# Four attention layers in one kernel: unit ends in pairs, outputs scaled in place, narrower masks, and unread matmuls in the final layer

## The chip, the cores and the metric

The kernel runs on one core of a Trainium2 chip. The time is that of the device, in microseconds, from one launch. It is compared by the median of several runs; a profile is one further execution, with its own time.

## What is computed

Four layers in a row work on x, of 2048 rows and 640 columns, in bfloat16. Each adds to x an attention over 32 heads of 20 columns, of x normalized by row. Layers 0 and 2 (weights A) let a row see itself and the 255 rows before it; layers 1 and 3 (weights B) let it see all 2048.

```python
def _A_ref(x, wqkv, wo):
    B, S, D = x.shape
    H = 32; Dh = D // H; W = 256
    qkv = (lambda x, *d: x.transpose(*d))((x @ wqkv).reshape(B, S, 3, H, Dh), 2, 0, 3, 1, 4)
    q, k, v = qkv[0], qkv[1], qkv[2]
    scores = jnp.einsum("bhqd,bhkd->bhqk", q, k) * (Dh ** -0.5)
    idx = jnp.arange(S)
    mask = (idx[:, None] - idx[None, :] >= 0) & (idx[:, None] - idx[None, :] < W)
    scores = jnp.where(mask[None, None], scores, -1e9)
    p = _softmax(scores, axis=-1)
    o = jnp.einsum("bhqk,bhkd->bhqd", p, v)
    return (lambda x, *d: x.transpose(*d))(o, 0, 2, 1, 3).reshape(B, S, D) @ wo
...
x = A_x
x = x + _A_ref(_layernorm(x, axis=-1), A_wqkv, A_wo)
x = x + _B_ref(_layernorm(x, axis=-1), B_wqkv, B_wo)
x = x + _A_ref(_layernorm(x, axis=-1), A_wqkv, A_wo)
x = x + _B_ref(_layernorm(x, axis=-1), B_wqkv, B_wo)
return x
```

`_B_ref` is the same without the mask.

## The kernel before, in words

**Units.** The 2048 queries are cut into four chunks of 512, the 32 heads into eight groups of four. A unit is one layer, chunk and group. A head's 20 columns lie in a strip of 32 partitions, so that four heads' scores (L1298) run side by side on TensorE's rows. Scores stand with keys on the partitions and queries on the columns, one bank of PSUM (512 columns) for each block of 128 keys and each head. In a layer with a window a bank holds two or more such blocks, those of the keys that the chunk can see (`window_banks`), and there is one bank for each of three patterns and each head.

**Tiles.** Banks of successive units are taken three at a time, now and then two or four: a tile. For each tile TensorE writes the scores, ScalarE takes the exponential of all its banks in one instruction (L1329) into `pt`, VectorE multiplies windowed banks by a mask of zeros and ones (L1399), and two or three tiles later TensorE multiplies by the values (L1363) into one bank, `op`. The values have a column of ones, so `op` holds, for each of four heads, 20 rows of sums and one row with the sum of the exponentials. Two halves of PSUM take turns: tile t uses banks 0 to 2, tile t+1 banks 3 to 5 or, with four, 3 to 6.

For a few banks of layers 1 and 3 the exponential is worked out on VectorE instead, in some twelve steps (`t_side`, L904 to L949).

**The end of a unit.** When the last value product of a unit is issued, `finish_unit` copies `op` to a tile `oT` in bfloat16 (L863, VectorE) and starts `t_tail`. This picks the sums with four small matmuls (L1044), takes reciprocals (L1049), splits each into a high and a low bfloat16 part (L1053, L1054), transposes them (L1061), copies the result (`rT`, L1063), spreads it over the partitions with four matmuls against `spread4` (L1072), and multiplies `oT` by it into `on` (L1079), which holds a chunk's eight groups. `require` forces work forward where something needs it.

**Projection.** When all groups of a chunk are done, `t_out` multiplies `on` with `wo` (L558) and adds to x (L567). With `packed`, here all of layer 3, `nu` is first moved by small copies on SyncE's queue (L1090) from strips of 32 to dense rows of 20, so that five matmuls do the work of eight. The last chunk of layer 3 does its first six groups apart (`t_before_last`) and the last two in the end. `load_wop` loads `wo`, dense or in strips, when the layer that projects changes.

**The order.** All engines take their instructions in an order that the program writes out, tile by tile. After a tile's scores and exponential are issued, `pump` issues as much of the waiting work as a credit allows: normalization (`t_ln`), projections of q, k and v (L370, L471), unit ends (`tails`, always first) and output projections. Such a piece takes one free bank of PSUM from `take_m`, and a wait of ("wait", n) lets n tiles pass. From layer 1 on that bank is mostly bank 6 alone. Units of layers 1 and 2, and 2 and 3, are interleaved; from chunk 1 of layer 3 on there is nothing left to interleave with.

**Unread matmuls.** `keep_clock` counts in `heat` how many full-size matmuls a tile has had. Below `least` it adds matmuls of a constant that nobody reads: into bank 6 at once where that is free (L640), or else into the first bank of a later tile, ahead of its scores (`owed`, L1292). What it aims at stands here:

```python
warmth = 1.76 if state["unit"] >= woven else 1.0
state["least"] = warmth * n_b / 3 if state["unit"] < index[3, 1, 0, None] else 0.0
state["floor"] = 0.9 if state["unit"] >= index[1, 1, 0, None] else 0.0
```

`woven` is the first unit of layer 1, so in layers 1 and 2 a tile of three banks has 1.76; from unit (3, 1, 0) on it has none, but for the fill matmuls of the very last unit's end (L1034).

Of the kernel before, what the change touches and what calls it, by code (L numbers as in the profile page):

```python
# [9 lines left out]
BF16 = mybir.dt.bfloat16  # L10
# [5 lines left out]
P = 128  # L16
# [33 lines left out]
def kernel(  # L50
# [22 lines left out]
    xtp = pool("xtp", 5)  # L73
    onp = pool("onp", 2)
    ptp = pool("ptp", 6)
    otp = pool("otp", 3)
    stp = pool("stp", 4)
    vsp = pool("vsp", 2)
    xnp = pool("xnp", 2)
# [19 lines left out]
    spread4 = big.tile([32, 4, P], BF16, name="spread4", tag="spread4")  # L99
# [28 lines left out]

    def packed(l, c):

        return l > 2

    def load_wop(w, dense):
        if dense:
            nc.sync.dma_start(out=wop[:, 0:KD, :], in_=wo_in[w].rearrange("(b p) f -> p b f", p=P))
            if w and out_n[0] == 12:
                v = wo_in[w].rearrange("(g j e) f -> j e g f", g=G, j=4)
                for j in range(4):
                    nc.sync.dma_start(
                        out=wop[32 * j : 32 * j + DH, G - 2 : G, :], in_=v[j][:, G - 2 : G, :]  # L140
                    )
# [27 lines left out]
    def other_constants():  # L169
        nc.vector.memset(op, 0.0)  # L170
        nc.vector.tensor_copy(
            out=sel4[:], in_=ident[:].rearrange("p (j m) -> p j m", j=4)[:, :, DH]
        )

        sp32 = rzp.tile([32, 2, 16], BF16, name="sp32", tag="sp32")
        nc.vector.tensor_copy(
            out=sp32[:], in_=ident[0:32, 0:32].rearrange("p (n r) -> p n r", n=2)
        )
        sp16 = rzp.tile([32, 16], BF16, name="sp16", tag="sp16")
        nc.vector.tensor_tensor(out=sp16[:], in0=sp32[:, 0, :], in1=sp32[:, 1, :], op=ALU.add)  # L180
        nc.vector.tensor_copy(
            out=spread4[:].rearrange("p q (j m) -> p (q j) m", m=32),
            in_=sp16[:].unsqueeze(2).to_broadcast((32, 16, 32)),
        )


    ready = set()
# [357 lines left out]
    def t_out(l, c):  # L545
        on = ons[l, c]
        last = (l, c) == (3, NC - 1)
        while last and "before_last" not in ready:
            yield ("wait", 1)
        assert out_seq[out_n[0]] == l % 2  # L550
        dense = packed(l, c) and not last
        a, b = (0, KD) if dense else (G - 2 if last else 0, G)
        for qb in range(4):
            for i in range(2):
                mb = yield from take_m()
                yp = ps[:, mb, 0:HD]
                for g in range(a, b):
                    nc.tensor.matmul(  # L558
                        yp, lhsT=on[:, g, qb * P : (qb + 1) * P],
                        rhs=wop[:, g, i * HD : (i + 1) * HD],  # L560
                        start=(g == a), stop=(g == b - 1),
                    )
# [12 lines left out]
        ready.add(("out", l, c))  # L575
        ready.add(("x", l + 1, c))
        n = out_n[0] = out_n[0] + 1
        if n < len(out_seq) and (n == 12 or out_seq[n] != out_seq[n - 1]):
            load_wop(out_seq[n], n >= 12)

    def t_before_last():

# [257 lines left out]
    def finish_unit(u):  # L840
# [10 lines left out]
        if (l, c) not in ons:  # L851
# [1 line left out]
                if len(ons) >= 2:  # L853
                    require(("out", ll, cc))
            ons[l, c] = onp.tile([P, G, C], BF16, name="on", tag="on")
        on = ons[l, c]
        while len(tails) >= 3:
            require(("tail", *tails[0].name[1:]))
        oT = otp.tile([P, C], BF16, name="oT", tag="oT")
        if u.part:  # L860
            nc.vector.tensor_tensor(out=oT[:], in0=part_o["t"][:, g, :], in1=op, op=ALU.add)
        else:
            nc.vector.tensor_copy(out=oT[:], in_=op)  # L863
        push_tail(("tail", l, c, g), t_tail(l, c, g, on, oT))


    aside = deque(u for u in units if u.aside)
    side_out = {}
# [158 lines left out]
        elif u.g == G - 1:  # L1027
            live["va"] -= 2 + 2 * (u.c > 0) + 2 * (u.c == NC - 1)

    def t_tail(l, c, g, on, oT):  # L1030
        def fill(count):

            for n in range(count * ((l, c, g) == (3, NC - 1, G - 1))):
                nc.tensor.matmul(  # L1034
                    ps[:, 0, :], lhsT=ident[:], rhs=masks[:, 0, :], start=True, stop=True
                )

        yield ("wait", 2)
        fill(2)
        mb = yield from take_m()  # L1040
        warm_bank(mb)
        zp = ps[:, mb, 0:16]
        for qb in range(4):
            nc.tensor.matmul(  # L1044
                zp[:, 4 * qb : 4 * qb + 4], lhsT=oT[:, qb * P : (qb + 1) * P],
                rhs=sel4[:], start=True, stop=True,
            )
        rz = rzp.tile([P, 16], F32, name="rz", tag="rz")
        nc.vector.reciprocal(out=rz[:], in_=zp)  # L1049
        drop_m(mb)  # L1050

        hl = rzp.tile([P, 2, 16], BF16, name="hl", tag="hl")
        nc.vector.tensor_copy(out=hl[:, 0, :], in_=rz[:])  # L1053
        nc.vector.tensor_tensor(out=hl[:, 1, :], in0=rz[:], in1=hl[:, 0, :], op=ALU.subtract)  # L1054
# [5 lines left out]
        rp = ps[0:32, mb, :].bitcast(BF16)[:, 0:P]  # L1060
        nc.tensor.transpose(out=rp, in_=hl[:].rearrange("p n r -> p (n r)"), identity=ident[:])  # L1061
        rT = rzp.tile([32, P], BF16, name="rT", tag="rT")
        nc.vector.tensor_copy(out=rT[:], in_=rp)  # L1063
        drop_m(mb)
        yield ("pe", 0.1)
        fill(1)
        yield ("wait", 2 if state["tick"] < last_tick[0] else 1)
        mb = yield from take_m()
        warm_bank(mb)
        zb = ps[:, mb, :]  # L1070
        for qb in range(4):
            nc.tensor.matmul(  # L1072
                zb[:, qb * P : (qb + 1) * P], lhsT=spread4[:, qb, :], rhs=rT[:],
                start=True, stop=True,
            )
        end = (l, c) == (3, NC - 1) and g >= G - 2
        spread = packed(l, c) and not end
        nu = on[:, 5 + g % 3 if spread else g, :]
        nc.vector.tensor_tensor(out=nu, in0=oT[:], in1=zb, op=ALU.mult)  # L1079
        drop_m(mb)  # L1080
        yield ("pe", 0.3)
        fill(3)
        if spread:
            yield ("wait", 2)
            for j in range(4):
                r, a = (4 * g + j) * DH, 0
                while a < DH:
                    b, o = divmod(r + a, P)
                    n = min(DH - a, P - o)
                    nc.sync.dma_start(  # L1090
                        out=on[o : o + n, b, :], in_=nu[32 * j + a : 32 * j + a + n, :]
                    )
# [93 lines left out]
    with tc.manual_schedule():  # L1186
# [72 lines left out]
        while ended is None or t < ended + 8:  # L1259
# [3 lines left out]
            if t < len(tiles) or banks:  # L1263
# [123 lines left out]
            if t > 0 and masked is not None:  # L1387
                cur_, pt_ = masked
                i = 0
                while i < len(cur_):  # L1390
# [49 lines left out]
```

## Time and profile before

| what | value |
|---|---|
| median of three runs | 2298.31 us (2295.11 to 2300.06) |
| the profiled execution | 2295.7 us |
| its span, first to last instruction | 2293.9 us |
| mean granted clock of TensorE | 0.865 |
| exponentials L1329 | 1645 instructions, 2105.8 us |
| scores L1298, full layers | 4008 matmuls, 451 ns each |
| masks L1399 | 403 instructions, 239.5 us |
| unread matmuls L640 | 655, 228.5 us |
| scaling L1079 | 128 instructions, 87.5 us |
| copy oT L863 | 112 instructions, 76.8 us |

The page's groups have busy time, the mean of one, and then the idle time of the engine just before them with what ended it. Busy times of one engine may overlap: an exponential's begins while the one before still drains, so a sum of durations is more than the time they occupy. A matmul's duration has its drain in it; several in a row end in much less than the sum. In a row of the waits the engine that waited stands first, then the one waited for, then the time in total, how often, and the longest. In the slices each digit is a tenth of busy share, for one fortieth of the span (57 us).

### The profile page before, as it was taken

The page shows a single profiled execution, that of the slowest core. Times are in us where ns is not written, and L with a number is a line of the kernel's source. Part 1 is how long each engine was busy: PE and PEld are TensorE (multiplying, and loading weights), DVE is VectorE, ACT ScalarE, POOL GpSimd, SP SyncE. Part 2 cuts the span into 40 slices and gives each one's busy share as a digit, 9 for nine tenths or more (in the row PEclk, how much of TensorE's full clock was granted, in tenths as well). Part 3 has the DMA queues.
Part 4 walks back from the last instruction along what each step waited for, and adds up shares of the span by engine and source line. Part 5 has one row for each costly group of instructions (what it writes and reads, how often), then busy time and mean ns, then how long its engine had stood idle before and what let it go on. Part 6 is the DMA issues. An engine that isn't in the chain of part 4 may idle for free.

```text
span 2293.9 us, 40624 instructions
## 1 busy us (share of the span) xinstructions
PE 1981.5 (86%) x15618; PEld 709.1 (31%) x15772; DVE 1468.5 (64%) x2736; ACT 2172.7 (95%) x1742; POOL 273.2 (12%) x445
## 2 busy tenths in 40 slices
PE   8889999989889888888888898898878888888887
PEld 3343343333233333233332333333222222222222
DVE  6777776436656666656676644452677877777772
ACT  6789899999999999999899999999999999999997
POOL 4323223200200112001220012002000000000000
PEclk9899999999999999999999999999765565556556
DMA  6223233321310223102330133103211111111100
GB/s 192 76 56 113 71 87 94 96 75 39 90 33 14 59 69 105 30 15 56 85 98 24 27 86 107 33 19 94 70 36 30 31 36 36 30 32 45 38 17 14
DMA packets 88809, 135.25 MB, mean 59 GB/s; under 512 B 21126, under 2 KB 64006, under 8 KB 88614
## 3 DMA queue, kind: packets, MB, share of 16 engines
q1 hardware_dynamic: 69398, 79.47, 13.0%
q0 software_dynamic: 19216, 53.17, 7.9%
q8 instruction: 124, 2.03, 0.4%
q14 instruction: 71, 0.58, 0.1%
HBM read 98.90 MB, written 27.79 MB: 55 GB/s over the span
## 4 chain that ended last, share of the span: by engine, by line
ACT 41%; PE 30%; issue 14%; DVE 13%; DMA 1%; POOL 0%; SPq 0%; ACTq 0%; another core or an unknown queue 0%; DVEq 0%; POOLq 0%
ACT pt L1329 40%; PE ps L1298 7%; PE ps L370 6%; PE ps L1363 5%; PE ps L558 4%; PE ps L471 3%; DVE pt L1399 3%; PE ps L640 2%; DVE st L320 1%; DVE on L1079 1%; DVE raw_o L911 1%; DVE oT L863 1%; ACT ka L1329 1%; PE ps L1292 1%; DVE x_sb L567 1%
## 5 line engine op out<-in xcount | busy, mean ns | idle before, releaser
L1329 ACT ACTIVATE pt<-ps 128x1536 bf16<-128x1536 f32 (+2 forms) x1645 | 2105.8, 1473 | 84.0 <-PE ps L1298 71.0
L1298 PE MATMUL ps<-qt,kt 32*128 32x512 bf16 x4008 | 637.5, 451 | 161.1 <-ACT pt L1329 130.2
L1363 PE MATMUL ps<-pt,vt 128*21 128x512 bf16 x3872 | 465.3, 452 | 5.9 <-issue 3.8
L1298 PEld LDWEIGHTS <-kt 32*128 32x128 bf16 x4008 | 182.5, 93 | 582.9 <-issue 562.6
L1399 DVE TENSOR_TENSOR pt<-pt,masks 128x1024 bf16<-128x1024 bf16 (+5 forms) x403 | 239.5, 626 | 120.9 <-ACT pt L1329 119.9
L640 PE MATMUL ps<-masks,ident 128*128 128x512 bf16 x655 | 228.5, 385 | 35.2 <-DVE rT L1063 9.2
L370 PE MATMUL ps<-xnT,wqk 128*128 128x512 bf16 x765 | 209.0, 384 | 19.1 <-issue 3.2
L1363 PEld LDWEIGHTS <-vt 128*21 128x21 bf16 x3960 | 99.7, 90 | 315.7 <-issue 304.8
L320 DVE CAST st<-ps 128x512 bf16<-128x512 f32 x134 | 92.5, 690 | 162.0 <-PE ps L370 157.5
L558 PE MATMUL ps<-wop,on 128*128 128x320 bf16 x904 | 161.0, 315 | 8.5 <-DVE x_sb L567 4.0
L1298 PE MATMUL ps<-qa,ka 32*128 32x384 bf16 (+2 forms) x1408 | 118.1, 278 | 27.9 <-ACT pt L1329 22.9
L911 DVE TENSOR_SCALAR xnT<-ps 128x512 int32<-128x512 f32 x88 | 60.8, 691 | 109.0 <-PE ps L904 108.8
L1079 DVE TENSOR_TENSOR on<-oT,ps 128x512 bf16<-128x512 bf16 x128 | 87.5, 683 | 55.5 <-PE ps L1072 51.8
L567 DVE TENSOR_TENSOR x_sb<-x_sb,ps 128x320 bf16<-128x320 bf16 x120 | 58.0, 483 | 95.8 <-PE ps L558 95.4
L471 PE MATMUL ps<-wv,xnT 128*128 128x320 bf16 x640 | 109.2, 300 | 8.4 <-DVE va L320 1.8
L863 DVE CAST oT<-ps 128x512 bf16<-128x512 f32 x112 | 76.8, 686 | 57.1 <-PE ps L1363 38.1
L558 PEld LDWEIGHTS <-on 128*128 128x128 bf16 x904 | 81.5, 101 | 74.7 <-issue 46.6
L370 PEld LDWEIGHTS <-wqk 128*128 128x128 bf16 x830 | 70.3, 97 | 109.0 <-issue 51.2
L640 PEld LDWEIGHTS <-ident 128*128 128x128 bf16 x743 | 57.9, 96 | 128.0 <-issue 126.2
L404 POOL TENSOR_SCALAR rstd<-mv 128x4 f32<-128x4 f32 x15 | 5.4, 363 | 740.7 <-DVE mv L391 738.7
L1363 PE MATMUL ps<-pt,va 128*21 128x384 bf16 (+2 forms) x1408 | 77.7, 282 | 4.2 <-DVE pt L1399 2.4
L1298 PEld LDWEIGHTS <-ka 32*128 32x128 bf16 x1408 | 43.2, 92 | 98.0 <-issue 89.4
(109 smaller groups left out, 1820.2 us busy)
## 6 DMA issues: line engine op xcount, KB each, us to landing
vt<-v_d SPq DMA_DIRECT2D x48, 336.0 KB
kt<-k_d SPq DMA_DIRECT2D x192, 80.0 KB
wqk<-in_B_wqkv_dram POOLq DMA_DIRECT2D x80, 160.0 KB, 3.6
wqk<-in_A_wqkv_dram POOLq DMA_DIRECT2D x70, 160.0 KB, 3.5
k_d<-st POOLq DMA_DIRECT2D x75, 128.0 KB, 2.3
q_d<-st POOLq DMA_DIRECT2D x75, 128.0 KB, 2.2
qt<-q_d SPq DMA_DIRECT2D x384, 20.0 KB
v_d<-vs POOLq DMA_DIRECT2D x16, 336.0 KB, 3.0
```

The lines of the kernel that those rows point to most:

```text
L320: nc.vector.tensor_copy(out=out_, in_=in_)
L370: nc.tensor.matmul(pq, lhsT=wt[:, dc, :], rhs=xt[:, dc, :], start=(dc == 0), stop=(dc == KD - 1),)
L471: nc.tensor.matmul(pv, lhsT=xt[:, dc, i * P : (i + 1) * P], rhs=wv_sb[l % 2][:, dc, h * HD : (h + 1) * HD], start=(dc == 0), stop=(dc == K ...
L558: nc.tensor.matmul(yp, lhsT=on[:, g, qb * P : (qb + 1) * P], rhs=wop[:, g, i * HD : (i + 1) * HD], start=(g == a), stop=(g == b - 1),)
L640: nc.tensor.matmul(ps[:, b, :], lhsT=ident[:], rhs=masks[:, 0, :], start=True, stop=True)
L863: nc.vector.tensor_copy(out=oT[:], in_=op)
L911: V.tensor_scalar(out=xi.bitcast(I32)[:, i * C : (i + 1) * C], in0=side["psum"], scalar1=SCALE * LOG2E * E23, scalar2=127.0 * E23, op0=ALU ...
L1079: nc.vector.tensor_tensor(out=nu, in0=oT[:], in1=zb, op=ALU.mult)
L1298: nc.tensor.matmul(sp[:, i, col * P : (col + qn) * P], lhsT=u.k(kc, j), rhs=u.q(j, q0, qn), start=True, stop=True,)
L1329: nc.scalar.activation(out=pt[:, i:k, b0 * P :], in_=sp[:, i:k, b0 * P :], func=ACT.Exp, scale=SCALE,)
L1363: nc.tensor.matmul(op[32 * j : 32 * j + VW, q0 * P : (q0 + qn) * P], lhsT=u.v(kc, j), rhs=pg[:, i, col * P : (col + qn) * P], start=(first ...
L1399: nc.vector.tensor_tensor(out=pt_[:, i:k, b0 * P :], in0=pt_[:, i:k, b0 * P :], in1=mv_, op=ALU.mult,)
```

## The change

It has five parts.

- **Pairs.** `finish_unit` gathers two units, and one `t_tail` ends both: sums of both into one 32-column block, one reciprocal, one cast, one subtraction, one transpose to 64 rows and one copy. `spread4` is built twice, on partitions 0 to 31 and 32 to 63, and `scaled` is then run for one unit after the other. A chunk's last group closes a pair; the last two units of all stay single. The output projection is pushed when all eight groups of its chunk are ready.
- **In place.** The pool `otp` is gone. `op` is copied straight into `on`, and the scaling reads and writes the same place.
- **Masks.** For the middle pattern (mask 1) only the middle two of four blocks are multiplied, instead of all four; in chunk 0 one block instead of two.
- **Unread matmuls.** `least` is no longer zero from unit (3, 1, 0) on.
- **Packing.** Chunk 0 of layer 3 is no longer packed; `wo` is loaded in strips for it and in dense form one chunk later, and the separate load of the last two groups goes.

```diff
     def packed(l, c):
 
-        return l > 2
+        return l == 3 and c > 0
...
             nc.sync.dma_start(out=wop[:, 0:KD, :], in_=wo_in[w].rearrange("(b p) f -> p b f", p=P))
-            if w and out_n[0] == 12:
-                v = wo_in[w].rearrange("(g j e) f -> j e g f", g=G, j=4)
-                for j in range(4):
-                    nc.sync.dma_start(
-                        out=wop[32 * j : 32 * j + DH, G - 2 : G, :], in_=v[j][:, G - 2 : G, :]
-                    )
             return
...
-        if n < len(out_seq) and (n == 12 or out_seq[n] != out_seq[n - 1]):
-            load_wop(out_seq[n], n >= 12)
+        if n < len(out_seq) and (n == 13 or out_seq[n] != out_seq[n - 1]):
+            load_wop(out_seq[n], n >= 13)
...
-        on = ons[l, c]
         while len(tails) >= 3:
-            require(("tail", *tails[0].name[1:]))
-        oT = otp.tile([P, C], BF16, name="oT", tag="oT")
+            require(tails[0].name)
+        end = (l, c) == (3, NC - 1) and g >= G - 2
+        oT = ons[l, c][:, 5 + g % 3 if packed(l, c) and not end else g, :]
         if u.part:
-            nc.vector.tensor_tensor(out=oT[:], in0=part_o["t"][:, g, :], in1=op, op=ALU.add)
+            nc.vector.tensor_tensor(out=oT, in0=part_o["t"][:, g, :], in1=op, op=ALU.add)
         else:
-            nc.vector.tensor_copy(out=oT[:], in_=op)
-        push_tail(("tail", l, c, g), t_tail(l, c, g, on, oT))
-
+            nc.vector.tensor_copy(out=oT, in_=op)
+        ended_units.append((l, c, g, oT))
+        if len(ended_units) == 2 or g == G - 1 or end :
+            push_tail(("tail", l, c, g), t_tail(list(ended_units)))
+            ended_units.clear()
+
+    ended_units = []
...
-    def t_tail(l, c, g, on, oT):
+    def t_tail(us):
+        final = us[-1][0:3] == (3, NC - 1, G - 1)
+
...
-        rz = rzp.tile([P, 16], F32, name="rz", tag="rz")
-        nc.vector.reciprocal(out=rz[:], in_=zp)
+        rz = rzp.tile([P, 2, 16], F32, name="rz", tag="rz")[:, 0:n, :]
+        nc.vector.reciprocal(out=rz.rearrange("p u r -> p (u r)"), in_=zp)
         drop_m(mb)
...
-        rT = rzp.tile([32, P], BF16, name="rT", tag="rT")
-        nc.vector.tensor_copy(out=rT[:], in_=rp)
+        rT = rzp.tile([64, P], BF16, name="rT", tag="rT")
+        nc.vector.tensor_copy(out=rT[0 : 32 * n], in_=rp)
         drop_m(mb)
         yield ("pe", 0.1)
         fill(1)
         yield ("wait", 2 if state["tick"] < last_tick[0] else 1)
+        for i in range(n):
+            yield from scaled(*us[i], 32 * i, rT, fill)
+        if any(packed(l, c) for l, c, g, oT in us):
+            yield ("wait", 2)
+        for u in us:
+            yield from settle(*u)
+
+    def scaled(l, c, g, oT, r, rT, fill):
         mb = yield from take_m()
         warm_bank(mb)
         zb = ps[:, mb, :]
         for qb in range(4):
             nc.tensor.matmul(
-                zb[:, qb * P : (qb + 1) * P], lhsT=spread4[:, qb, :], rhs=rT[:],
-                start=True, stop=True,
+                zb[:, qb * P : (qb + 1) * P], lhsT=spread4[r : r + 32, qb, :],
+                rhs=rT[r : r + 32, :], start=True, stop=True,
             )
-        end = (l, c) == (3, NC - 1) and g >= G - 2
-        spread = packed(l, c) and not end
-        nu = on[:, 5 + g % 3 if spread else g, :]
-        nc.vector.tensor_tensor(out=nu, in0=oT[:], in1=zb, op=ALU.mult)
+        nc.vector.tensor_tensor(out=oT, in0=oT, in1=zb, op=ALU.mult)
         drop_m(mb)
...
         if g == G - 1:
+            while any(("tail", l, c, n) not in ready for n in range(G)):
+                yield ("wait", 1)
             need = first_use(l + 1, c, 0) if l < 3 else len(units) + c
...
-                warmth = 1.76 if state["unit"] >= woven else 1.0
-                state["least"] = warmth * n_b / 3 if state["unit"] < index[3, 1, 0, None] else 0.0
+                state["least"] = (1.76 if state["unit"] >= woven else 1.0) * n_b / 3
                 state["floor"] = 0.9 if state["unit"] >= index[1, 1, 0, None] else 0.0
...
                     if m is not None:
-                        mv_ = masks[:, m, b0 * P :].unsqueeze(1).to_broadcast(
-                            (P, k - i, C - b0 * P)
+                        cols = slice(max(b0, m == 1) * P, 3 * P if m == 1 else C)
+                        mv_ = masks[:, m, cols].unsqueeze(1).to_broadcast(
+                            (P, k - i, cols.stop - cols.start)
                         )
                         nc.vector.tensor_tensor(
-                            out=pt_[:, i:k, b0 * P :], in0=pt_[:, i:k, b0 * P :], in1=mv_,
-                            op=ALU.mult,
+                            out=pt_[:, i:k, cols], in0=pt_[:, i:k, cols], in1=mv_, op=ALU.mult
                         )
```

More of the change, by code (lines that the diff above doesn't have):

```diff
@@ L75 @@
     ptp = pool("ptp", 6)
-    otp = pool("otp", 3)
     stp = pool("stp", 4)
@@ L98 @@
     sel4 = big.tile([P, 4], BF16, name="sel4", tag="sel4")
-    spread4 = big.tile([32, 4, P], BF16, name="spread4", tag="spread4")
+    spread4 = big.tile([64, 4, P], BF16, name="spread4", tag="spread4")
     masks = big.tile([P, 3, C], BF16, name="masks", tag="masks")
@@ L173, in other_constants @@
         )
[L175 to L184, printed above, removed]
+        sp32 = rzp.tile([64, 2, 16], BF16, name="sp32", tag="sp32")
+        sp16 = rzp.tile([64, 16], BF16, name="sp16", tag="sp16")
+        for u in range(2):
+            r = slice(32 * u, 32 * u + 32)
+            nc.vector.tensor_copy(
+                out=sp32[r], in_=ident[r, r].rearrange("p (n r) -> p n r", n=2)
+            )
+            nc.vector.tensor_tensor(
+                out=sp16[r], in0=sp32[r, 0, :], in1=sp32[r, 1, :], op=ALU.add
+            )
+            nc.vector.tensor_copy(
+                out=spread4[r].rearrange("p q (j m) -> p (q j) m", m=32),
+                in_=sp16[r].unsqueeze(2).to_broadcast((32, 16, 32)),
+            )
     ready = set()
@@ L1028, in pv_emitted @@
             live["va"] -= 2 + 2 * (u.c > 0) + 2 * (u.c == NC - 1)
-    def t_tail(l, c, g, on, oT):
+    def t_tail(us):
+        final = us[-1][0:3] == (3, NC - 1, G - 1)
         def fill(count):
-            for n in range(count * ((l, c, g) == (3, NC - 1, G - 1))):
+            for n in range(count * final):
                 nc.tensor.matmul(
@@ L1036, in fill @@
                 )
+        n = len(us)
         yield ("wait", 2)
@@ L1041, in t_tail @@
         warm_bank(mb)
[L1042 to L1047, printed above, removed]
-        rz = rzp.tile([P, 16], F32, name="rz", tag="rz")
-        nc.vector.reciprocal(out=rz[:], in_=zp)
+        zp = ps[:, mb, 0 : 16 * n]
+        for i, (l, c, g, oT) in enumerate(us):
+            for qb in range(4):
+                a = 16 * i + 4 * qb
+                nc.tensor.matmul(
+                    zp[:, a : a + 4], lhsT=oT[:, qb * P : (qb + 1) * P],
+                    rhs=sel4[:], start=True, stop=True,
+                )
+        rz = rzp.tile([P, 2, 16], F32, name="rz", tag="rz")[:, 0:n, :]
+        nc.vector.reciprocal(out=rz.rearrange("p u r -> p (u r)"), in_=zp)
         drop_m(mb)
-        hl = rzp.tile([P, 2, 16], BF16, name="hl", tag="hl")
-        nc.vector.tensor_copy(out=hl[:, 0, :], in_=rz[:])
-        nc.vector.tensor_tensor(out=hl[:, 1, :], in0=rz[:], in1=hl[:, 0, :], op=ALU.subtract)
+        hl = rzp.tile([P, 2, 2, 16], BF16, name="hl", tag="hl")[:, 0:n]
+        nc.vector.tensor_copy(out=hl[:, :, 0, :], in_=rz)
+        nc.vector.tensor_tensor(out=hl[:, :, 1, :], in0=rz, in1=hl[:, :, 0, :], op=ALU.subtract)
         yield ("pe", 0.25)
@@ L1059, in t_tail @@
         warm_bank(mb)
-        rp = ps[0:32, mb, :].bitcast(BF16)[:, 0:P]
-        nc.tensor.transpose(out=rp, in_=hl[:].rearrange("p n r -> p (n r)"), identity=ident[:])
-        rT = rzp.tile([32, P], BF16, name="rT", tag="rT")
-        nc.vector.tensor_copy(out=rT[:], in_=rp)
+        rp = ps[0 : 32 * n, mb, :].bitcast(BF16)[:, 0:P]
+        nc.tensor.transpose(
+            out=rp, in_=hl.rearrange("p u n r -> p (u n r)"), identity=ident[:]
+        )
+        rT = rzp.tile([64, P], BF16, name="rT", tag="rT")
+        nc.vector.tensor_copy(out=rT[0 : 32 * n], in_=rp)
         drop_m(mb)
@@ L1082, in t_tail, with settle @@
         fill(3)
-        if spread:
-            yield ("wait", 2)
+    def settle(l, c, g, oT):
+        on = ons[l, c]
+        if packed(l, c) and not ((l, c) == (3, NC - 1) and g >= G - 2):
             for j in range(4):
@@ L1090, in t_tail @@
                     nc.sync.dma_start(
-                        out=on[o : o + n, b, :], in_=nu[32 * j + a : 32 * j + a + n, :]
+                        out=on[o : o + n, b, :], in_=oT[32 * j + a : 32 * j + a + n, :]
                     )
```

## The prediction

> **What bounds the kernel now.** I read the page's engine shares and its 40 slices first, then the busy times by stretch, then who waits for whom in each stretch, and last the timeline of a few microseconds.
>
> ```profile
> PE 1981.5 (86%) x15618; PEld 709.1 (31%) x15772; DVE 1468.5 (64%) x2736; ACT 2172.7 (95%) x1742; POOL 273.2 (12%) x445
> ...
> ACT  6789899999999999999899999999999999999997
> ...
> PEclk9899999999999999999999999999765565556556
> ```
>
> ScalarE is busy for 95% of the span, and the slices say that this is no average over unlike stages: from about slice 5 to slice 39 it stands at 9. What ScalarE does there is the exponentials (L1329). So the time is ScalarE's work plus the gaps between its instructions, and only the gaps can be won. The clock row shows something else: TensorE has its clock nearly full until slice 28 and about half of it afterwards, in the last layer.
>
> ```profile
> 400.00:1640.00 1240.00, 1084.94 (x8945) 411.62 (x9057) 702.19 (x1364) 1199.50 (x927) 151.17 (x232) 0.99 0.23 60
> 1640.00:2283.00 643.00, 530.25 (x3356) 141.40 (x3354) 468.92 (x686) 633.55 (x464) 0.00 (x0) 0.56 0.11 31
> 2283.00:2294.00 11.00, 6.11 (x35) 2.74 (x34) 5.47 (x14) 0.00 (x0) 0.00 (x0) 0.81 0.18 62
> ```
>
> These are busy times of three stretches (PE, weight loads, DVE, ACT, POOL, then the granted clock). In the middle stretch ScalarE is idle for 40 us of 1240 at clock 0.99; in the last layer, 1640 to 2283, it is idle for 9.5 us of 643 at clock 0.56. So the half clock costs ScalarE almost nothing. The gaps of the last layer have one cause, in the list of waits for 1640 to 2283; the second line is the same row for 400 to 1640:
>
> ```profile
> ACT pt L1329 <- PE ps L1298: 8.7, 16, 1.2
> ```
>
> ```profile
> ACT pt L1329 <- PE ps L1298: 34.8, 84, 1.6
> ```
>
> The timeline shows how such a gap arises, and what ScalarE does without one:
>
> ```profile
> 1869.71 1.51 PE L558 MATMUL ps<-wop,on 128*128 128x320 bf16 x5
> ...
> 1872.41 1.45 ACT L1329 ACTIVATE pt<-ps 128x1536 bf16<-128x1536 f32 x1 [0.61 <-PE ps L1298]
> ```
>
> ```profile
> 1792.14 20.62 ACT L1329 ACTIVATE pt<-ps 128x1536 bf16<-128x1536 f32 x15
> ```
>
> The first: five output-projection matmuls at half clock (1.51 us) sit between the scores of two tiles, and ScalarE runs dry for 0.61 us. The second: 15 three-bank tiles take 20.6 us; the first overlaps the end of a wider one, so I take 1.343 us a tile from the steps between TensorE's releases in that row. That is ScalarE's own pace, and runs in the warm stretch have it too (five tiles in 6.82 us, 1.45 of it the first). A faster TensorE doesn't speed up the exponential; it only closes gaps.
>
> **Unread matmuls in the last layer.** The order of instructions of both kernels gives 747 more unread matmuls after the first score of chunk 1 of layer 3: 303 into bank 6 and 444 "owed" ones, ahead of the scores of a later tile. Their number follows the rule of the layers before (1.76 weighted matmuls per three banks), where the clock is 0.99, so I expect the last layer near 1.0 instead of 0.56. Cost of one: five back-to-back 512-column matmuls end after 1.24 us in the warm stretch (1404.13, L370), 0.215 us with the ends taken off; 747 of them are 161 us of TensorE. Does that fit? I counted all matmuls between one tile's scores and the next, each at the warm slot (0.215 us for 512 columns, a third of it for a score, a fourth for a value product): before, a tile of the last layer holds 0.59 us; after, 0.85; the middle stretch has 0.84 to 0.87. The limit is 1.343. At half clock the 0.59 are 1.18 us, so the changed layer has more slack, not less. What stays are dense tiles, those over 1.1 us: 27 in the last layer against 212 from the end of layer 0 to 1640. There 212 such tiles go with some 37 us of ScalarE gaps, 0.17 each, so I keep 27 x 0.17 = 4.7 of the 8.7 us: **-4.0 us**; bounds 0 and -8.7.
>
> The Trainium skill speaks against this part: TensorE: Matmul & The Clock Gate, "HAM oscillation — how this bites in real kernels", says that the clock falls when TensorE has idle gaps of more than some 3.4 us. The longest wait of TensorE's matmuls in this stretch is 1.2 us, so by the rule the layer would already be at full clock, the 747 matmuls would be load alone, and this part would be worth 0 or cost time. The row has 0.56 with TensorE's matmuls busy for 530 of 643 us. The row decides[...].
>
> **The end.** After 2283 ScalarE does nothing; the chain is last value product, copy, the sums, reciprocal, transpose, spread, scale, projection, store: 11 us. It is entered cold: value products 0.60 us where warm ones take 0.40, and the three fill matmuls of L1034 1.44 us, just ahead of the transpose. **-0.8 us** for these; bounds 0 and -1.5. The last two units are not paired, so their chain keeps its steps.
>
> **Ends in pairs.** For 63 of the 65 new ends two units share a reciprocal, a cast, a subtraction and a copy on VectorE and a transpose on TensorE:
>
> ```profile
> L1049 DVE RECIPROCAL rz<-ps 128x16 f32<-128x16 f32 x128 | 32.6, 255 | 36.2 <-PE ps L1044 35.4
> L1063 DVE COPY rT<-ps 32x128 bf16<-32x128 bf16 x128 | 26.6, 208 | 47.7 <-PE ps L1061 46.8
> L1053 DVE CAST hl<-rz 128x16 bf16<-128x16 f32 x128 | 23.6, 184 | 4.4
> L1054 DVE TENSOR_TENSOR hl<-rz,hl 128x16 bf16<-128x16 f32 x128 | 22.4, 175 | 4.4
> ```
>
> 63 x (0.255+0.208+0.184+0.175) = 52 us off VectorE (a little less, the pair's being twice as wide). The scaling in place has the same 128 multiplications of 0.683 us.
>
> **Narrower masks.** 403 instructions as before, over 311,296 columns instead of 368,640. By the rows of 512 columns (416 ns) and 1536 (950 ns) a column is 0.52 ns: 30 us off VectorE. The nearest rows for the new shapes are the 256-column ones (277 ns), on the same line.
>
> VectorE thus loses some 80 of 1468 us, and nearly all of it lies beside ScalarE's work. Worth something is only what makes TensorE, which works in order, late:
>
> ```profile
> PE ps L640 <- DVE rT L1063: 9.2, 17, 1.2
> ...
> PE ps L640 <- DVE st L320: 6.3, 15, 0.9
> PE ps L640 <- DVE on L1079: 5.2, 14, 0.8
> ```
>
> (waits of TensorE, 400 to 1640). All such rows from 0 to 1640 sum to 62.5 us without the first memset. Waits on rT and rz are 14.6 of them and come half as often: -7.3. Waits on masks (3.2 for TensorE, 2.8 for ScalarE) shrink by 12%: -0.7. The other 44.7 us shrink with VectorE's load, 7% less there: -3.1. Of these 11.1 us I take half for ScalarE, since a tile has slack: **-5.5 us**; bounds 0 and -11.
>
> **What the pair adds.** A unit's end waits for the next unit, and only the projection of a chunk (L558) needs it. Its first matmuls now stand behind two multiplications in a row instead of one: 0.68 us more in VectorE's queue at each of 12 chunks, with the next tile's scores queued behind them on TensorE. Bounds 0 and +8.2; before, L558 waited for such a multiplication for 2.6 us in all, so I take **+1.5 us**. In chunk 0 of layer 3 the packing goes: 36 small copies fewer on SyncE's queue and 24 more 320-column matmuls (24 x 0.14 = 3.2 us of TensorE, in bursts of 8 not 5); nothing taken, up to +2. The dense load of wo comes one chunk later, with no reader near. The wide tiles of four banks grow from 22 to 30, at 1.77 us against 1.343 for three: -0.2. The three extra constants stand before the bound begins: 0.
>
> **Sum:** -4.0 - 0.8 - 5.5 + 1.5 - 0.2 = -9.0 us. The profiled execution took 2295.7 us (span 2293.9, 1.8 around it), so 2286.7. The median of the runs shown is 2298.3, 2.6 above it: on that footing **2289 us**. 0.2%, or 4.6 us, is about what can be told from no change here.
>
> **Rivals.**
>
> *A, the unread matmuls make ScalarE wait (chance 0.10).* In the changed order 90 of the 303 in bank 6 wait for VectorE to have read that bank. TensorE stops there, and the next scores stand behind. VectorE in this layer is 73% busy with operations of up to 1.22 us, so one wait can be over 1 us, against a slack of some 0.49 us (1.343 - 0.853). Each excess is a gap. From 0.10 us of gap on average (9.0/90) nothing is left of the gain; at 0.24 it is +21.6 - 9.0 = +13, **2311**. For it: in the middle stretch the unread matmuls are what waits for VectorE (rows above). Against: the rows of L640 on VectorE sum to 25 us over 276 waiting ones, 0.09 each, inside the slack.
>
> *B, nothing to see (0.14).* ScalarE's pace is the floor, the gaps move, dense tiles stay dense: final layer -2, the rest 0: **2296**. For it: the count of dense tiles before 1640 hardly changes (212 and 207).
>
> *C, the relief of VectorE pays early (0.18).* From 99 to 112 us ScalarE waits 10 us in four gaps, the longest of 4.4, since VectorE is behind with masks, statistics and ends, and TensorE then runs cold. Of the 34 us of gaps from 100 to 400 a third goes, of those to 1640 a quarter, of the last layer's 6: -11 - 9 - 6 plus the rest above, **2272**. Against: TensorE is 92% busy from 100 to 400, and its work there stays.
>
> **From these the numbers.** The likeliest case has 0.58, its own range 2284 to 2295. The range 2275 to 2300 takes in B, most of C and A's beginning. Faster by over 0.2% (below 2293.7): 0.54 of the likeliest, C, and a little of B, 0.74; slower by as much: A, 0.10; the rest 0.16.
>
> **What would show it.** Granted clock near 1.0 from 1640 on; ScalarE's waits for the scores there about 5 us; about 52 and 30 us less for the ends and the masks on VectorE; TensorE's waits on rT halved; waits of L558 on the multiplication up by a few us. A clock that stays near 0.6, or waits of unread matmuls on VectorE that turn into gaps of ScalarE, would make it wrong; so would gaps before 400 that halve.

## The result, and the profile after

The changed kernel takes 2289.31 us (median of four runs, 2286.27 to 2290.19), the one before 2298.72 (four runs): a ratio of 0.9959, 95% interval 0.9942 to 0.9976, or 9.4 us less (5 to 13). The forecast was 2289. That agreement is worth less than it looks: by the medians of the experiments three of its terms were off by 5 to 10 us each and cancelled, which is luck.

The page of the changed kernel, with the engines and the slices that were shown of before:

```profile
PE 1994.6 (87%) x16267; PEld 732.7 (32%) x16493; DVE 1410.9 (62%) x2486; ACT 2172.8 (95%) x1740; POOL 273.7 (12%) x445
...
ACT  7789899999999989999899999999999999999998
...
PEclk9999999999999999999999999999999999999999
```

ScalarE's busy time is what it was (2172.7 before), so all of the gain is in its gaps. VectorE is busy for 58 us less. The clock's half-speed stage is gone. Stretches after 85 us, of the kernel before and then of the kernel after (busy us of PE, weight loads, DVE, ACT and POOL, the granted clock, and DMA):

```profile
85.00:136.00 51.00, 40.43 (x384) 17.98 (x387) 39.97 (x103) 33.11 (x34) 11.48 (x16) 0.83 0.20 55
136.00:1620.00 1484.00, 1315.70 (x11184) 509.35 (x11321) 884.37 (x1759) 1423.76 (x1132) 229.20 (x352) 1.00 0.24 65
1640.00:2275.00 635.00, 524.25 (x3320) 140.07 (x3318) 468.92 (x686) 626.05 (x459) 0.00 (x0) 0.56 0.11 32
```

```profile
85.00:136.00 51.00, 43.89 (x448) 19.77 (x451) 41.72 (x106) 37.88 (x40) 9.70 (x15) 0.87 0.18 52
136.00:1620.00 1484.00, 1317.04 (x11097) 505.41 (x11238) 833.16 (x1564) 1420.93 (x1127) 229.24 (x349) 0.99 0.23 65
1640.00:2275.00 635.00, 536.30 (x3993) 167.03 (x4054) 463.47 (x640) 628.22 (x458) 0.00 (x0) 0.98 0.11 33
```

In the 51 us at the end of the first chunk ScalarE gets 4.8 us more done; in the next 1484 us it gets 2.8 us less done, though VectorE has 51 us less to do there; in the last 635 us 2.2 us more.

A finer ruler: every unit ends with one copy of `op` (L861 or L863 before, L858 or L860 after), 128 in all and in the same order. Where they start, in us from the span's start, numbered from 0:

| unit end | before | after | difference |
|---|---|---|---|
| 6 | 83.14 | 82.16 | -1.0 |
| 11 | 135.88 | 129.39 | -6.5 |
| 56 | 809.39 | 802.28 | -7.1 |
| 57 | 839.76 | 837.61 | -2.1 |
| 103, the last before chunk 1 of layer 3 | 1625.42 | 1621.62 | -3.8 |
| 127, the last | 2283.20 | 2278.01 | -5.2 |
| span | 2293.9 | 2288.4 | -5.5 |

In these two executions everything was won by 136 us, some of it was lost again in the middle, and the last layer gave only 1.4 us. How some of the first part was won is in the timelines. Before, TensorE's projection waits for the scaling (`on`) for 2.37 us, then runs at a granted clock of 0.50 (its eight matmuls take 2.29 us), and ScalarE has nothing for 4.36 us:

```profile
106.06 2.29 PE L558 MATMUL ps<-wop,on 128*128 128x320 bf16 x8 [2.37 <-DVE on L1079]
...
108.93 1.02 ACT L1329 ACTIVATE pt<-ps 128x1024 bf16<-128x1024 f32 x1 [4.36 <-PE ps L1298]
```

After, VectorE is less behind, the wait is 0.85 us, the eight matmuls run at a clock of 1.00 (1.25 us), and ScalarE's gap is 1.18 us:

```profile
103.34 1.25 PE L555 MATMUL ps<-wop,on 128*128 128x320 bf16 x8 [0.85 <-DVE on L1092]
...
104.95 1.02 ACT L1346 ACTIVATE pt<-ps 128x1024 bf16<-128x1024 f32 x1 [1.18 <-PE ps L1315]
```

### The profile page after: what moved, and what is told of

It reads as the page before. It is cut to its first block, busy times and chain, and to the rows that moved or that the text cites. A ratio compares the mean times of both kernels' runs of the same rounds, so it can differ in the third digit from the quotient of the medians.

```text
span 2288.4 us, 41718 instructions
## 1 busy us (share of the span) xinstructions
PE 1994.6 (87%) x16267; PEld 732.7 (32%) x16493; DVE 1410.9 (62%) x2486; ACT 2172.8 (95%) x1740; POOL 273.7 (12%) x445
## 3 DMA queue, kind: packets, MB, share of 16 engines
q1 hardware_dynamic: 68878, 79.43, 12.6%
## 4 chain that ended last, share of the span: by engine, by line
ACT 43%; PE 28%; issue 16%; DVE 10%; DMA 1%; POOL 1%; ACTq 0%; SPq 0%; DVEq 0%; POOLq 0%
ACT pt L1346 41%; PE ps L1315 7%; PE ps L367 5%; PE ps L1379 4%; PE ps L555 4%; PE ps L468 3%; PE ps L637 2%; DVE pt L1416 2%; ACT ka L1346 2%; DVE on L1092 1%; DVE st L317 1%; PE ps L1309 1%; DVE x_sb L564 1%; PE ps L432 1%; PE ps L1088 1%
## 5 line engine op out<-in xcount | busy, mean ns | idle before, releaser
L1315 PE MATMUL ps<-qt,kt 32*128 32x512 bf16 x4008 | 548.2, 387 | 70.7 <-ACT pt L1346 53.3
L1379 PE MATMUL ps<-pt,vt 128*21 128x512 bf16 x3840 | 396.3, 389 | 8.5 <-issue 4.5
L637 PE MATMUL ps<-masks,ident 128*128 128x512 bf16 x982 | 339.7, 391 | 41.2 <-DVE on L1092 9.8
L1315 PEld LDWEIGHTS <-kt 32*128 32x128 bf16 x4008 | 160.1, 91 | 447.6 <-issue 430.6
L1416 DVE TENSOR_TENSOR pt<-pt,masks 128x1024 bf16<-128x1024 bf16 (+6 forms) x403 | 209.5, 554 | 141.9 <-ACT pt L1346 141.4
L1309 PE MATMUL ps<-masks,ident 128*128 128x512 bf16 x476 | 160.3, 385 | 79.6 <-ACT pt L1346 55.1
L367 PE MATMUL ps<-xnT,wqk 128*128 128x512 bf16 x761 | 207.2, 384 | 19.5 <-DVE on L1092 4.1
L555 PE MATMUL ps<-wop,on 128*128 128x320 bf16 x928 | 154.7, 300 | 9.9 <-DVE x_sb L564 6.6
L637 PEld LDWEIGHTS <-ident 128*128 128x128 bf16 x1101 | 81.9, 97 | 183.2 <-issue 180.6
L468 PE MATMUL ps<-wv,xnT 128*128 128x320 bf16 x640 | 112.3, 304 | 8.3 <-DVE on L1092 3.1
L1092 DVE TENSOR_TENSOR on<-on,ps 128x512 bf16<-128x512 bf16 x128 | 86.4, 684 | 52.3 <-PE ps L1088 51.9
L860 DVE CAST on<-ps 128x512 bf16<-128x512 f32 x112 | 77.0, 688 | 67.3 <-PE ps L1379 46.3
L367 PEld LDWEIGHTS <-wqk 128*128 128x128 bf16 x830 | 70.0, 97 | 111.6 <-issue 54.2
L555 PEld LDWEIGHTS <-on 128*128 128x128 bf16 x928 | 80.1, 97 | 71.0 <-issue 47.0
L1309 PEld LDWEIGHTS <-ident 128*128 128x128 bf16 x514 | 47.5, 96 | 135.8 <-issue 130.5
```

Of the source, the lines that this page charges most:

```text
L367: nc.tensor.matmul(pq, lhsT=wt[:, dc, :], rhs=xt[:, dc, :], start=(dc == 0), stop=(dc == KD - 1),)
L468: nc.tensor.matmul(pv, lhsT=xt[:, dc, i * P : (i + 1) * P], rhs=wv_sb[l % 2][:, dc, h * HD : (h + 1) * HD], start=(dc == 0), stop=(dc == K ...
L555: nc.tensor.matmul(yp, lhsT=on[:, g, qb * P : (qb + 1) * P], rhs=wop[:, g, i * HD : (i + 1) * HD], start=(g == a), stop=(g == b - 1),)
L637: nc.tensor.matmul(ps[:, b, :], lhsT=ident[:], rhs=masks[:, 0, :], start=True, stop=True)
L1092: nc.vector.tensor_tensor(out=oT, in0=oT, in1=zb, op=ALU.mult)
L1309: nc.tensor.matmul(sp[:, 0, :], lhsT=ident[:], rhs=masks[:, 0, :], start=True, stop=True)
```

## The experiments

One profiled execution is one draw. The runs of one kernel lie 4 to 19 us apart, so medians of several runs are compared; ratios are to the runs of before on the same chip. Three sets of four kernels were run: their medians of before are 2299.16, 2298.09 and 2297.80. A ratio can lie 1 in 1000 off the quotient of the two medians, so an amount in us below is good to a few us.

### Unread matmuls alone, and taken away

The first kernel is the one before with this edit, the second the one after with its reverse:

```diff
-                warmth = 1.76 if state["unit"] >= woven else 1.0
-                state["least"] = warmth * n_b / 3 if state["unit"] < index[3, 1, 0, None] else 0.0
+                state["least"] = (1.76 if state["unit"] >= woven else 1.0) * n_b / 3
```

> The kernel before, with unread matmuls in the last layer as well and nothing else changed. Theory 1 (the prediction's sum): the gaps of ScalarE in the last layer shrink by 4.0 us and the end by 0.8, so 4.8 us less than before, 2294. Theory 2 (read from the two traces, whose unit ends lie 6.5 us apart by 136 us of the span and 5.2 at the last one): the last layer gives only 1 to 1.5 us, 2297.5. The granted clock from 1640 on is near 0.98 in both.

> The kernel after, without the unread matmuls of the last layer. Theory 1: they are worth 4.8 us, so 2294. Theory 2: 1 to 1.5 us, so 2290.5. The clock of the last layer falls back to about 0.55 in both.

Alone on before: 2289.49 us, ratio 0.9947 (0.9929 to 0.9965). Taken from after: 2298.35, ratio 0.9987 (0.9977 to 0.9997). By the medians this part is worth 9.7 us on one kernel and 9.0 on the other, twice theory 1 and far from theory 2, which had trusted one pair of traces. On before the interval (8 to 16 us) leaves out both theories; taken from after, the ratios say 6 us, and theory 1's 4.8 isn't excluded. The stretch of the last layer in the first kernel (unread matmuls on before):

```profile
1640.00:2283.00 643.00, 543.59 (x4091) 174.13 (x4157) 478.11 (x703) 642.61 (x472) 0.00 (x0) 1.00 0.12 33
```

and ScalarE's waits there:

```profile
ACT pt L1329 <- PE ps L1298: 0.2, 1, 0.2
```

Before, this row has 8.7 us. From unit end 103 to 127 the kernel takes 646.8 us instead of 657.8; nothing of the dense tiles' gaps is left. The second kernel, at a clock of 0.55 again, takes 662.5, the kernel after 656.4. That the first kernel's profiled span (2295.9) is longer than that of before comes from the middle: there it has a stretch at clock 0.86 from 600 to 700 us, where its program is that of before.

### Narrower masks alone, and wide masks put back

The edit of the masks alone, on before, and its reverse on after:

```diff
-                        mv_ = masks[:, m, b0 * P :].unsqueeze(1).to_broadcast(
-                            (P, k - i, C - b0 * P)
+                        cols = slice(max(b0, m == 1) * P, 3 * P if m == 1 else C)
+                        mv_ = masks[:, m, cols].unsqueeze(1).to_broadcast(
+                            (P, k - i, cols.stop - cols.start)
                         )
```

> The kernel before with the narrower masks alone: 30 us less for VectorE. Theory 1: waits on masks shrink by 0.7 us and the other waits on VectorE by about 1.1, half of it seen by ScalarE, so about 1 us less, 2297.5. Theory 2: VectorE is the bound from 85 to 136 us, and masks are about half of what it is relieved of by then, so 3 us less, 2295.5, with the gain there by unit end 11.

> The kernel after with the wide masks of before: 30 us more for VectorE. Theory 1: about 1 us more, 2290.5. Theory 2: 3 us more, 2292.5, lost by 136 us of the span.

Alone on before: 2292.37, ratio 0.9960 (0.9944 to 0.9975). Wide masks on after: 2299.42, ratio 1.0002 (0.9989 to 1.0016). So 6.8 us by the medians on before and 10.1 on after, more than either theory said (the interval on before is 6 to 13 us). Brought to one clock, as below, it is about 8 us on either kernel. The trace of the first has unit end 11 at 131.96 (3.9 us earlier than before) and unit end 31 at 386.95 (7.0 earlier); past that, 103 lies 3.1 earlier. In this pair of traces the gain is made in layer 0, which ends with unit end 31, but not all by 136 us.

If these parts add up, the rest of the change (pairs, scaling in place, unpacking) must cost 9.7 + 6.8 - 9.4 = 7.1 us by the medians. That became theory 3.

### Without the rest; with single ends; pairs early or late

The first is before with both edits above. The others are the kernel after with one line changed; for single ends:

```diff
-        if len(ended_units) == 2 or g == G - 1 or end :
+        if True:
```

For pairs only in chunks 0 and 1 of layer 0, and for pairs only after them, the condition keeps its form and gets one more term:

```diff
+        if len(ended_units) == 2 or g == G - 1 or end or (l, c) > (0, 1):
...
+        if len(ended_units) == 2 or g == G - 1 or end or (l, c) <= (0, 1):
```

> The kernel before with the unread matmuls of the last layer and the narrower masks: the change without pairs, scaling in place and unpacking. The four runs so far read so: unread matmuls are worth 9 to 10 us on either kernel, masks 7 to 10, and what is left of the change costs 6 to 10. Theory 3 (the rest of the change loses): 9.7 + 6.8 less than before, 2282.5, and below the kernel after. Theory 2 (the two parts share one gain, the pairs cost nothing): as the kernel after, 2289.

> The kernel after with each unit ended alone; scaling in place, unpacked chunk 0, masks and unread matmuls stay. Theory 3a (pairing is what loses, by two multiplications in a row that TensorE waits for): as the kernel before with unread matmuls and masks, 2282.5, with TensorE's waits on on near 13 us again up to 1620 and those on rT back near 8 to 11. Theory 3b (scaling in place or unpacking lose, pairing helps): at or above 2289.

> The kernel after with pairs in chunks 0 and 1 of layer 0 only. Theory 3a with theory 2's early gain (pairs relieve VectorE where it is the bound, and cost later): the best of the three, 2280. If pairs cost everywhere: above the kernel with single ends. If pairing helps everywhere: 2292.

> The kernel after with single ends in chunks 0 and 1 of layer 0 and pairs afterwards. Theory 3a with an early gain: the worst, 2292. If pairs cost everywhere: 2287. If pairing is of no account at all: as the other two.

| kernel | median us | ratio to before (95%) |
|---|---|---|
| unread matmuls and masks only | 2282.52 | 0.9938 (0.9919 to 0.9958) |
| after, single ends | 2285.09 | 0.9948 (0.9931 to 0.9966) |
| after, pairs only early | 2276.67 | 0.9913 (0.9897 to 0.9929) |
| after, pairs only late | 2291.20 | 0.9977 (0.9968 to 0.9986) |
| after | 2289.31 | 0.9959 (0.9942 to 0.9976) |

Theory 3a fits the medians, with the early gain. Without pairs the parts add up to 2282.5, as reckoned. Against single ends, pairs in the first two chunks win 8.4 us (2285.1 to 2276.7) and pairs afterwards cost 6.1 (2285.1 to 2291.2). The two don't add: beside late pairs the early ones win only 1.9 (2291.2 to 2289.3), beside early pairs the late ones cost 12.6. The intervals set early pairs alone apart from single ends, from late pairs and from after, and late pairs alone from single ends; single ends and after they don't set apart. The version with early pairs alone is the fastest of the case that an interval sets apart from after. Scaling in place and unpacking (2282.5 against 2285.1) can't be told from nothing.

Much of these amounts goes with the clock. Within a kernel the time follows the mean granted clock (last section), and the kernels had different ones: a median of 0.9885 with single ends, 0.993 with early pairs, 0.986 with late pairs and in after. Brought to one clock at 1.4 us for each 0.001, an estimate from those runs, 1 to 2 us is left of the 8.4, 3 to 4 of the 6.1 and 2 to 3 of the 12.6. The traces with narrow masks say about the same. Unit end 11 starts at 130.4 us on average in six with early pairs (129.2 to 133.4) and at 132.7 in five without (131.9 to 133.7). From there to unit end 103 four with late pairs take 1489.1 to 1492.2 us and five with single ends 1487.1 to 1489.5. Whether pairs change the clock or these executions drew it isn't shown: late pairs had 0.981 to 0.989 in 21 runs, single ends 0.982 to 0.992 in ten, and early pairs alone have four runs.

What do late pairs do? Of TensorE's waits from 136 to 1620 us, these are the rows on the scaling (`on`) and the first on `rT`, in the kernel with single ends and then in the kernel after:

```profile
PE ps L637 <- DVE rT L1071: 7.4, 13, 1.2
PE ps L637 <- DVE on L1092: 3.8, 10, 0.8
PE ps L367 <- DVE on L1092: 1.6, 3, 1.0
PE ps L468 <- DVE on L1092: 1.1, 2, 0.7
PE ps L555 <- DVE on L1092: 0.3, 1, 0.3
```

```profile
PE ps L637 <- DVE on L1092: 7.5, 16, 2.1
PE ps L468 <- DVE on L1092: 2.4, 3, 1.2
PE ps L367 <- DVE on L1092: 1.9, 4, 1.0
PE ps L555 <- DVE on L1092: 1.8, 4, 0.6
PE ps L637 <- DVE rT L1071: 0.7, 2, 0.5
```

The waits on `rT` nearly vanish, and those on the scaling double, from 6.8 to 13.6 us, the longest from 1.0 to 2.1. Mostly it isn't the output projection (L555) that waits, but what takes the bank next: unread matmuls (L637) and projections (L367, L468). All of TensorE's waits on `rT`, `rz` and the scaling together are 18.8 us with single ends and 17.4 after, so their sum doesn't explain the loss; that the longer single waits do is argued, not shown.

In the last layer the kernel after has stretches of some 4 us at a lower clock (near 1676, 1720, 1880, 1944 and 2100); 10 of ScalarE's 14 gaps there, 5.3 of 6.3 us, come in them:

```profile
ACT pt L1346 <- PE ps L1315: 6.3, 14, 1.0
```

In the traces of after with single ends and with early pairs there are none between 1624 and 2264. But the kernel with unread matmuls and masks only, which has single ends too, has three (near 1872, 1888 and 2248), so such falls don't belong to late pairs alone. One of them, in the kernel after, by pieces of 4 us:

```profile
2100.00:2104.00 4.00, 2.44 (x13) 0.51 (x13) 1.90 (x2) 3.70 (x4) 0.00 (x0) 0.79 0.00 0
2104.00:2108.00 4.00, 4.00 (x16) 0.59 (x15) 0.69 (x1) 2.93 (x3) 0.00 (x0) 0.50 0.00 0
2108.00:2112.00 4.00, 4.00 (x19) 0.77 (x19) 3.72 (x6) 2.82 (x3) 0.00 (x0) 0.50 0.02 4
```

and in its timeline:

```profile
2102.05 1.47 ACT L1346 ACTIVATE pt<-ps 128x1536 bf16<-128x1536 f32 x1
...
2104.60 1.03 PE L1309 MATMUL ps<-masks,ident 128*128 128x512 bf16 x2
2105.57 0.61 PE L1315 MATMUL ps<-qt,kt 32*128 32x512 bf16 x3
...
2106.29 2.96 ACT L1346 ACTIVATE pt<-ps 128x1536 bf16<-128x1536 f32 x2 [1.02 <-PE ps L1315]
```

In the piece in which the clock begins to fall TensorE is busy for 2.44 of 4 us; then the clock is 0.50, and the unread matmuls that were to hold it add to the delay: two of them take 1.03 us ahead of the scores, where two take 0.59 at full clock, and ScalarE waits 1.02 us.

### Tiles of four banks, and a gap between the two scalings

Three of those falls come right after a tile of four banks, of which after has 30 and the kernel with single ends 22. Two kernels without such tiles (`size = 4` made 3; on after and on early pairs), one with more of them (`not tails` struck from the condition; on single ends), and one that lets two tiles pass between the two scalings of a pair:

```diff
         for i in range(n):
+            if i:
+                yield ("wait", 2)
             yield from scaled(*us[i], 32 * i, rT, fill)
```

> The kernel after without tiles of four banks (before has 22, after 30, the kernel with single ends 22). In the traces of after every fall of the clock in the last layer at 1720, 1944 and 2100 follows a tile of four banks, and the unread matmuls that then run at half clock stand ahead of the scores. Theory W (these wide tiles leave TensorE too little to do[...]): the last layer, from unit end 103 to 127, goes from 656.4 to 647 to 649 us with no stretch of 4 us under 0.95, and the time to 2282. Theory P (the pairs do it in another way): the last layer stays near 655, the time near 2289.

> Pairs in chunks 0 and 1 of layer 0 only, without tiles of four banks. Theory W: nothing left to win in the last layer, the 22 wide tiles were worth some 0.02 us each, 2276 to 2278. Theory P: the same. If it is over 2280, wide tiles are worth more than their pace says.

> The kernel after with single ends, and with tiles of four banks allowed while a unit's end is under way: 39 of them instead of 22. Theory W: falls of the clock after wide tiles as in the kernel after, the last layer 652 to 656 us instead of 647.1, the time near 2292. Theory P: no more falls than with 22, 647 us and 2285.

> The kernel after with two more tiles between the two scalings of a pair; by that 26 wide tiles instead of 30. Theory G (two multiplications close together are what TensorE waits for in the middle): its waits on on from 136 to 1620 fall from 13.6 to about 7 us, the stretch from unit end 11 to 103 from 1492 to 1489 us; the time 2286. Otherwise the waits only move and the time stays at 2289.

| kernel | median us | ratio to before (95%) | ends 103 to 127 in its trace, us |
|---|---|---|---|
| after, no wide tiles | 2286.65 | 0.9953 (0.9936 to 0.9970) | 650.4 |
| early pairs, no wide tiles | 2281.75 | 0.9930 (0.9905 to 0.9955) | 652.3 |
| single ends, 39 wide tiles | 2282.47 | 0.9937 (0.9920 to 0.9955) | 649.9 |
| after, a gap in the pair | 2279.24 | 0.9922 (0.9893 to 0.9950) | 654.1 |

Theory W falls. After without wide tiles has 650.4 us in the last layer of its trace instead of 656.4, but its time can't be told from that of after; with 39 wide tiles single ends are no slower, and early pairs without any have the clock fall in the last layer (near 1776, 1964, 1992, 2076 and 2088). A wide tile can come just before a fall, but the falls don't need one.

The gap is worth 10 us by the medians: 2289.3 to 2279.2, about what leaving out the late pairs gives. The intervals of the two overlap; at one clock, by the estimate above, 6 us is left. TensorE's waits on the scaling from 136 to 1620 go from 13.6 to 8.7 us, as theory G said, if not to 7; all rows on it:

```profile
PE ps L637 <- DVE on L1094: 6.1, 12, 1.3
PE ps L367 <- DVE on L1094: 1.2, 2, 1.0
PE ps L468 <- DVE on L1094: 0.8, 2, 0.5
PE ps L555 <- DVE on L1094: 0.6, 2, 0.4
```

Its profiled execution doesn't show the shorter middle, since it is the slowest of its six runs (2290.2) and took 291.4 us from unit end 56 to 72, where after takes 280.8, with the clock at 0.66 from 860 to 900; so a gain is likely, and the path from waits to time is argued.

## Why the prediction came true, by its steps

**ScalarE as the bound: right.** In every trace its busy time is the same within a few us, and the gaps make the difference.

**Clock near 1.0 in the last layer: right** (0.98 and 1.00 against 0.56). Here the Trainium skill's rule of no idle gaps over some 3.4 us (TensorE: Matmul & The Clock Gate, "HAM oscillation — how this bites in real kernels") had stood against the row, and the row held: with unread matmuls on before the clock goes from 0.56 to 1.00, though TensorE's matmuls are busy for 544 of 643 us instead of 530. Why the clock was low is not shown: the narrow shapes of those matmuls are one reading; another is too little work, by the prediction's count 0.59 us of a 1.343 us tile at full clock before and 0.85 after. No run separates them.

**Its worth: too small by half.** The term was -4.0 and -0.8; alone it measures -9.7. What failed is the count of dense tiles: 27 of them, at 0.17 us of gap each, were to leave 4.7 us, and with unread matmuls on before 0.2 us were left. The 0.17 came from stretches where dense tiles stand beside waits on VectorE; which of the two made those gaps wasn't tested, but in the last layer dense tiles alone cost nothing. In the trace of after 6.3 us are left, near the forecast, but most of them from falls of the clock that it didn't have. The end was 10.7 us from the last copy and is 10.3: -0.4 for -0.8.

**Masks: too small by a factor of seven or more.** 30 us off VectorE were right (239.5 to 209.5):

```profile
L1416 DVE TENSOR_TENSOR pt<-pt,masks 128x1024 bf16<-128x1024 bf16 (+6 forms) x403 | 209.5, 554 | 141.9 <-ACT pt L1346 141.4
```

Their worth was put at 0.7 us plus a share of the other waits, about 1 us; it is 6.8 to 10.1. The step that failed spread VectorE's relief over the whole kernel by the waits that TensorE showed. In layer 0 VectorE is itself late, and a wait of 2.4 us for it there becomes 4.4 us without scores. That was rival C's mechanism, at a third of its size: ScalarE's idle time from 100 to 400 us goes from 34.0 to 29.7 us with the masks alone and to 31.0 after, where C took a third off.

**Pairs: wrong sign where they are late.** The four rows on VectorE fell by 42.6 us where 52 had been reckoned, most of the difference from the reciprocal: twice as wide it takes 355 ns for 255, so two cost 155 ns less, not 255. Here in the kernel after:

```profile
L1055 DVE RECIPROCAL rz<-ps 128x32 f32<-128x32 f32 x63 | 22.4, 355 | 34.9 <-PE ps L1050 33.0 <-ACT pt L1346 1.0 <-ACT va L315 0.8
```

Waits on `rT` were to halve and went from 11.4 to 1.3 us (0 to 1620). The added wait was sought at L558, for up to +8.2 and taken at +1.5; L555 waits on the scaling for 2.6 us, as before. It came at bank 6: waits on the scaling went from 13.2 to 18.3 us. In all, TensorE's waits on VectorE fell by 8.6 us where 11.1 had been reckoned. In the sum the pairs stood for some -3 us (half of 7.3 and of about 2, plus the 1.5); measured, late pairs cost 6.1 us and early ones win 8.4, much of both going with the clock, and both together cost 4.2 (2285.1 to 2289.3), which can't be told from nothing. So the step that took half of TensorE's waits for ScalarE's gaps failed: the waits fell and no gain came of it.

**The sum** was right since 5 us too little for the unread matmuls and 6 to 9 for the masks met with some 10 us too much for the rest: by luck, not by its steps.

**Rival A** had the right place and the wrong cause: with unread matmuls on before TensorE's waits on VectorE from 1640 to 2264 go from 3.3 to 8.1 us and ScalarE's gaps from 8.7 to 0.2, so those waits don't reach it; unread matmuls do delay it when the clock falls under them. **Rivals B and C** (2296 and 2272) lie outside the interval of the result.

**Open:** what starts a fall of the clock in one execution and not in the next. Wide tiles aren't needed for it. Open too is how much of what pairs cost or win comes by way of the clock.

## What to carry to other kernels

Where one engine is the bound and the rest is gaps, price an edit stage by stage: 30 us off an engine was worth 7 to 10, most of it made in the stage where that engine was late, and what pairs took off it where it wasn't late brought no time. When small pieces are merged, ask what takes their buffer next: here two tiles between two results that pass through the same bank went with 6 to 10 us less. Before a difference of some us is put down to an edit, see whether the clock differs too. And if the sum of a forecast comes true, run the parts alone before believing them.

## What the runs showed of the hardware

The spread between runs of one kernel goes with the clock. Over the 21 runs with late pairs the time goes from 2286.0 us at a mean granted clock of 0.989 to 2301.1 at 0.981, with a correlation of -0.97 and 1.65 us for each 0.001; over the 10 and 14 runs with single ends and with wide masks it is 1.4 and 1.8 us (-0.96 and -0.99); over all twelve kernels made for the experiments but the one with four runs, 1.0 to 1.8 us (-0.78 to -0.99). As 0.001 of 2290 us is 2.3 us of full clock, or 4.6 us at half clock, each microsecond at half clock goes with some 0.2 to 0.4 us more time, an estimate, in a kernel whose bound is another engine. That the clock is the cause, and not the stalls that lower it, these runs don't show.
